# Attention and two mixture-of-experts layers on one core: second-layer products at other places of the second MoE's steps, with the banks swapped from step to step

## The chip, the cores and the metric

One core of a Trainium2 chip. The metric is the device time of the whole program in microseconds (us). The core's engines run beside each other, each through its own list of instructions in order: PE (TensorE, matrix products into the accumulators, PSUM), DVE (VectorE), ACT (ScalarE), POOL (GpSimd) and SP (SyncE, which issues the transfers). They wait for each other at semaphores.

## The reference

```
x = attention(q, k, v)                     # 4 x 576 tokens, 8 heads of 64; to (2304, 512)
p = domain_probs / (domain_probs.sum(-1) + 1e-9)
y = 0
for e in range(4):                         # first MoE: 512 -> 1024 -> 512
    y += p[:, e:e+1] * (relu(x @ w1[e]) @ w2[e])
h = y @ w_in                               # second MoE: 512 -> 2048 -> 512
g = where(h > 0, h, exp(min(h, 0)) - 1)    # ELU
out = g @ w_out
```

All in fp32. The kernel writes each factor as a sum of a high and a low part and forms hi\*hi, hi\*lo and lo\*hi, three matrix products for one.

## The kernel before

Expert 0 runs beside the attention. The rest is a list of 30 *steps*, `STEPS` = (s, b): s counts ten slices of 512 hidden units (s = 0 to 5 the first MoE, 6 to 9 the second; `S_MOE` = 6), b three blocks of 768 tokens. The step with number i = 3s + b forms the *first layer* of its slice and block, and between its products the *second layer* of the step before, i - 1.

**First layer** (`product`, `PRODUCTS`, L1146). A 2 x 2 block product by Strassen's scheme in Winograd's form: seven products, done for two halves of the slice (`fp` 0 and 1), so 14 products a step, numbered 0 to 13 (`idx = 7 * fp + p`), each of six 128x128x384 matmuls. Each half has four PSUM banks A to D. Product 0 goes to C, from which ACT takes a copy `s5` (L1424). Product 1 goes to B, and ACT copies B to A (L1427, "the copy to A" below). Product 2 adds to B, so it must not start before that copy has read B. Then DVE writes D = B + s5 (L1431), product 3 adds to A, product 4 to B, DVE writes C = B + s5 (L1442), product 5 adds to D, product 6 to B. So A, C, D and B end in turn as the four quarters A11, A22, A21, A12 of the hidden layer. The second half's bank D is the bank that the next step's product 1 overwrites. In `fp` 1 the same things happen at products 7 to 13: product 8 is followed by the copy to A, and 9 waits for it.

**ELU** (`elu`, second MoE). For a quarter, ACT does three operations (L1184 to L1186) and, later in the order, `rest()` does two on DVE (L1193, L1194; the second reads the bank). After A21, `rest()` also forms the sums S1, S2, S3 (L1198 to L1200) and after A12 S4 (L1203), which the second layer's seven-product scheme needs. Each result is split in a high part by ACT (L1168) and a low part by POOL (L1169). `run_pend()` is where the DVE part is put in the order: at product 4, 5, 6 and the next half's 0, or earlier, at product 3 or 10, if a second-layer product stands behind that one (`if idx in fill: run_pend()`).

**Second layer.** For s = 7, 8, 9 it has seven *turned products* T0 to T6 (`turned_product`, `TURNED`, L1272), of twelve matmuls each, into two pairs of PSUM banks called X and Y, which they use in turn: T0, T2, T4, T6 go to Y and T1, T3, T5 to X. T0, T1 and T5 start a pair afresh, the others add to what is there. Behind each, DVE adds the pair to the result in SBUF (L1281, "the add"); the next product of the same pair must not start before that add has read it. In the order of DVE the add stands behind what the next first-layer product brings (`flush_adds()`). `PLACES` = (1, 2, 4, 6, 8, 10, 12) says behind which first-layer products T0 to T6 stand. For s = 6 the second layer is eight plain groups (`group`, `GROUP_PLACES`), for s = 5 six chunks (`chunk`).

**Weights.** Some 24 small jobs a step, the *hooks*, prepare the next weights: `MIXED` and `PLAIN` say how many of them have been put into the order by the end of each product (hooks 2 and 3 behind product 1, hooks 10 to 12 behind 6, and so on). For s > 6 `w2_fast` holds the second-layer weights' sums (`w2_sum`, DVE, L807) and splits (`w2_parts`, ACT L798 and POOL L799), and `w1_steps` the first layer's: `hi` on ACT (L757), `lo` and `sums1` on DVE (L768, L773, L774) or POOL, `sums2` on POOL. Steps with b = 0 carry most of `w2_fast` and the second half of `w1_steps`, b = 1 the end of `w2_fast`, b = 2 the first half of `w1_steps` for the next s. The last step has no hooks. The instructions of each engine stand in the order in which this code emits them; nothing moves them later.

Of the kernel before, what the change touches and what calls it, by code (L numbers as in the profile page):

```python
# [21 lines left out]
def tile_attention_moe_moe(  # L22
# [50 lines left out]
    def cut(*sizes):  # L73
# [5 lines left out]
    TB, FS = 384, 4  # L79
    NB = NT // (2 * TB)  # L80
    STEPS = [(s, b) for s in range((NU - 1) * FPU // FS) for b in range(NB)]
    S_MOE = (E - 1) * FPU // FS
# [19 lines left out]


    TURNED = (
        ("A11", "B11", "Y", (0, 0)), ("S1", "T1", "X", (1, 1)), ("S2", "T2", "Y", (0, 1)), ("S4", "B22", "X", (0, 1)),
        ("S3", "T3", "Y", (1, 1)), ("A12", "B21", "X", (0, 0)), ("A22", "T4", "Y", (1, 0)),
    )
    STARTS, ENDS = (0, 1, 5), (3, 4, 5, 6)
    GROUPS = tuple((th, m) for th in (1, 0) for m in range(4))
    GROUP_PLACES = (2, 3, 4, 6, 8, 9, 11, 12)  # L110

    const = ctx.enter_context(tc.tile_pool(name="const", bufs=1))
    big = ctx.enter_context(tc.tile_pool(name="big", bufs=1))
# [624 lines left out]
    def w1_steps(s, p):  # L738

        r, t = [], []  # L740

        def begin():
            r.append(w1r.pop((s, p)).rearrange("p j (d f) -> p j d f", d=KD))
            for _ in range(4):
                t.append(wp.tile([P, 2, KD, P], F32R, tag="w1", name="w1s"))
            if s % 2:
                t[0], t[2] = t[2], t[0]
            hi(0)

# [25 lines left out]

        def sums2():
            f1, f2 = r[0][:, 0], r[0][:, 1]
            nc.gpsimd.tensor_tensor(out=f2[:, 2:], in0=f2[:, 2:], in1=f1[:, :2], op=ALU.subtract)
            nc.gpsimd.tensor_tensor(out=f1[:, 2:], in0=f1[:, 2:], in1=f2[:, 2:], op=ALU.subtract)

        return {
            -5: begin, -4: lambda: lo(0), -2: sums1, -1: lambda: hi(1), 0: lambda: lo(1), 1: sums2,
            5: lambda: hi(2), 6: lambda: lo(2), 8: lambda: hi(3), 9: lambda: lo(3),
        }
# [24 lines left out]
    def w2_fast(i, s, d):  # L809

        for k, fn, op in (
            (8, w2_parts, "B11"), (14, w2_sum, "T1"), (16, w2_parts, "T1"), (18, w2_parts, "B22"), (19, w2_sum, "T3"),
            (21, w2_parts, "B21"), (25, w2_sum, "T2"), (27, w2_parts, "T2"), (30, w2_parts, "T3"), (31, w2_sum, "T4"),
            (34, w2_parts, "T4"),
        ) if s > S_MOE else (
            (8, w2_parts, "B11"), (13, w2_sum, "T1"), (17, w2_parts, "T1"), (18, w2_parts, "B22"), (19, w2_sum, "T3"),
            (21, w2_parts, "B21"), (22, w2_parts, "T3"), (24, w2_sum, "T2"), (26, w2_parts, "T2"), (27, w2_sum, "T4"),
            (30, w2_parts, "T4"),
        ):
            put = lambda k, fn: at2(i, k, fn) if k >= 0 else at(210 + k, fn)  # L820
            put(k - d, lambda fn=fn, op=op: fn(s, op))
# [55 lines left out]
    for i, (s, b) in enumerate(STEPS):  # L877
# [7 lines left out]
        if b == 0:  # L885
# [11 lines left out]
            if s == S_MOE:  # L897
                a1, b1 = (42, 42)
            elif s > S_MOE:
                a1, b1 = (34, 39)  # L900
            if more and not SEVEN[s] and not SEVEN[s + 1]:
                at2(i, a2, lambda s=s: w_load(s + 1, 0, 1))
                at2(i, b2, lambda s=s: w_load(s + 1, 1, 1))
# [353 lines left out]
    def turned_product(i, k, last=False):  # L1257
# [3 lines left out]
            for n in "XY":  # L1261
                sums[n] = bank("o")
        s, b = STEPS[i]
        op, wname, x, (th, mh) = TURNED[k]
        t, y = w2g[s, wname], sums[x][:, :, :TB]
        for m in range(2):
            n = 0
            for fp in range(2):
# [69 lines left out]
    def second_product(i, k):  # L1338
# [60 lines left out]
    pieces = [piece for u, bi, (f,) in pending for piece in second_(u, bi, f)]  # L1399

    for i, (s, b) in enumerate(STEPS):
        fill = {}
        if fast(i - 1):
            one = turned_product if turned(i - 1) else second_product
            fill = {n: (one, i - 1, k) for k, n in enumerate(PLACES)}
        elif turned(i - 1):
            fill = {n: (group, i - 1, *g) for g, n in zip(GROUPS, GROUP_PLACES)}
        elif i > 0:
            fill = {n: (chunk, i - 1, c) for c, n in zip(CHUNKS, (1, 3, 5, 8, 10, 12))}
        hooks = MIXED if fast(i - 1) or turned(i - 1) else PLAIN  # L1410
        if i + 1 == len(STEPS):
            hooks = {}
        for fp in range(2):
            A_, B_, C_, D_ = (A, B, C, D) if fp == 0 else (C, D, A, B)
            banks = {"A": A_, "B": B_, "C": C_, "D": D_}
            f1, f2 = 2 * fp, 2 * fp + 1
            moe = s < S_MOE
            for p in range(len(PRODUCTS)):
                idx = 7 * fp + p
                goal[0] = i * SH + hooks[idx] if idx in hooks else hook2_n[0]  # L1420
# [121 lines left out]
```

## Time and profile before

| | us |
|---|---|
| median of 3 runs | 1254.12 (1252.95 to 1254.65) |
| the profiled execution's own time | 1253.47 |
| its span | 1251.6 |

The profiled execution is one run, and the span is what its trace covers; 1.9 us lie around it. All moments below count from the start of the span. The first layer of the step with s = 6, b = 0 begins at 801.7, the first step that carries turned products (s = 7, b = 1) at 953.4; the last step ends at 1226.1, and behind it stand the last seven turned products alone. A matmul's end is modelled in the trace, so a product's length is best read from start to start.

### The profile page before, as it was taken

The numbers are of one execution on the slowest core, as the hardware profiler recorded it, in microseconds if no ns is written. First come the engines' busy times: TensorE is split into PE (matmuls) and PEld (weight loads), VectorE is DVE, ScalarE is ACT, GpSimd is POOL, SyncE is SP. The second block draws the span as 40 slices with busy tenths as digits, with TensorE's granted clock in tenths as the row PEclk, the third lists the DMA queues.
The fourth block names the chain that finished last, engine by engine and source line by source line (L and its number), as shares of the span: only waits on it lengthen the run. The fifth ranks groups of instructions, "written<-read, shape, count | busy, mean of one in ns | idle before, by whom it ended". The sixth has DMA issues, their size and how long they took to land.

```text
span 1251.6 us, 21084 instructions
## 1 busy us (share of the span) xinstructions
PE 1184.6 (95%) x7516; PEld 1126.3 (90%) x7516; DVE 906.8 (72%) x1516; ACT 676.1 (54%) x1430; POOL 651.1 (52%) x611
## 2 busy tenths in 40 slices
PE   7799999999999999999999999978999988989897
PEld 6788889889999999999999998868999977988897
DVE  6877887565877887877877865655557788787774
ACT  6544543244455554454554534546777656665662
POOL 4522552046476476575584632536247557556652
PEclk9999999999999999999999999989999989999898
DMA  9345557837777767676766679978655554644152
GB/s 268 109 143 171 187 196 245 307 116 258 251 254 253 248 243 261 224 247 241 245 247 244 218 279 325 322 233 262 239 182 193 206 194 168 231 157 173 53 225 89
DMA packets 157400, 272.35 MB, mean 218 GB/s; under 512 B 12784, under 2 KB 83952, under 8 KB 157296
## 3 DMA queue, kind: packets, MB, share of 16 engines
q1 hardware_dynamic: 155568, 267.87, 62.5%
q10 hardware_dynamic: 1728, 3.15, 0.7%
q8 instruction: 59, 0.97, 0.3%
q14 instruction: 45, 0.37, 0.1%
HBM read 224.83 MB, written 46.14 MB: 216 GB/s over the span
## 4 chain that ended last, share of the span: by engine, by line
PE 73%; DVE 12%; ACT 7%; issue 3%; DMA 3%; POOL 2%; SPq 0%; DVEq 0%; ACTq 0%; POOLq 0%
PE o L1361 18%; PE h L1146 13%; PE m L1146 13%; PE o L1272 7%; PE h L1005 7%; PE o L1005 6%; ACT half L1185 1%; DVE gt L1199 1%; DVE accs L1281 1%; DVE extra L1193 1%; PE o L1245 1%; PE o L1247 1%; PE o L1246 1%; DVE half L1200 1%; DVE half L1194 1%
## 5 line engine op out<-in xcount | busy, mean ns | idle before, releaser
L1146 PE MATMUL m<-xh,w1s 128*128 128x384 f32 x840 | 250.0, 341 | 12.1 <-DVE half L1194 7.8
L1146 PE MATMUL h<-xh,w1s 128*128 128x384 f32 x840 | 244.6, 337 | 9.9 <-DVE half L1194 6.2
L1146 PEld LDWEIGHTS m<-xh,w1s 128*128 128x128 f32 x840 | 156.3, 190 | 20.6 <-DVE half L1194 10.6
L1146 PEld LDWEIGHTS h<-xh,w1s 128*128 128x128 f32 x840 | 155.4, 189 | 12.5 <-DVE half L1194 6.5
L1146 PE MATMUL m<-xl,w1s 128*128 128x384 f32 x420 | 141.8, 338 | 0.0
L1146 PE MATMUL h<-xl,w1s 128*128 128x384 f32 x420 | 141.1, 336 | 0.0
L1005 PE MATMUL o<-w2t,hpa 128*128 128x512 f32 x432 | 118.4, 401 | 0.8 <-DVE hpa L1037 0.5
L1005 PE MATMUL h<-xh,w1t 128*128 128x256 f32 (+1 forms) x512 | 112.0, 297 | 0.1
L1005 PEld LDWEIGHTS h<-xh,w1t 128*128 128x128 f32 x512 | 86.1, 192 | 5.2 <-POOL w1t L442 0.3
L1361 PE MATMUL o<-w2g,xh 128*128 128x256 f32 x540 | 90.4, 282 | 0.0
L799 POOL TENSOR_TENSOR w2g<-r,w2g 128x512 fp32r<-128x512 f32 x56 | 75.8, 1362 | 26.1 <-ACT w2g L798 26.1
L1005 PEld LDWEIGHTS o<-w2t,hpa 128*128 128x128 f32 x432 | 75.6, 189 | 14.9 <-DVE hpa L1037 2.4
L1361 PE MATMUL o<-w2g,hpa 128*128 128x256 f32 x540 | 89.0, 282 | 0.0
L1361 PE MATMUL o<-w2g,xl 128*128 128x256 f32 x540 | 87.3, 282 | 0.0
L1383 DVE SCALAR_TENSOR_TENSOR accs<-o,pn,accs 128x256 f32<-128x256 f32 x180 | 75.7, 474 | 14.8 <-PE o L1361 14.2
L1146 PEld LDWEIGHTS m<-xl,w1s 128*128 128x128 f32 x420 | 79.8, 190 | 0.4
L1146 PEld LDWEIGHTS h<-xl,w1s 128*128 128x128 f32 x420 | 79.5, 189 | 0.5
L1361 PEld LDWEIGHTS o<-w2g,xh 128*128 128x128 f32 x540 | 78.0, 190 | 0.1
L1005 PE MATMUL h<-xl,w1t 128*128 128x256 f32 (+1 forms) x256 | 77.3, 302 | 0.0
L1361 PEld LDWEIGHTS o<-w2g,hpa 128*128 128x128 f32 x540 | 76.1, 190 | 0.1
L1361 PEld LDWEIGHTS o<-w2g,xl 128*128 128x128 f32 x540 | 75.6, 190 | 0.2
L1272 PE MATMUL o<-hpa,w2g 128*128 128x384 f32 x216 | 53.5, 366 | 19.9 <-DVE accs L1281 19.9
(301 smaller groups left out, 3033.7 us busy)
## 6 DMA issues: line engine op xcount, KB each, us to landing
xh<-xs SPq DMA_DIRECT2D x210, 384.0 KB, 5.3
xl<-xs SPq DMA_DIRECT2D x210, 384.0 KB, 6.0
r<-in_w_dram SPq DMA_DIRECT2D x56, 256.0 KB, 4.7
xs<-stage SPq DMA_DIRECT2D x43, 256.0 KB, 3.1
xs<-xh SPq DMA_DIRECT2D x21, 384.0 KB, 4.1
xs<-xl SPq DMA_DIRECT2D x21, 384.0 KB, 4.1
r<-scratch SPq DMA_DIRECT2D x24, 256.0 KB, 4.1
x<-in_w_in_dram SPq DMA_DIRECT2D x10, 512.0 KB, 3.8
```

Of the source, the lines that this page charges most:

```text
L799: nc.gpsimd.tensor_tensor(out=t[:, 1], in0=src, in1=t[:, 0].bitcast(F32), op=ALU.subtract)
L1005: nc.tensor.matmul(out, lhsT, rhs, **kw)
L1146: nc.tensor.matmul(dst, t[:, wl, c + dl, :], x[xl_][:, dl, :], start=(n == 0 and p < 2), stop=(n == 5), skip_group_check=True,)
L1185: nc.scalar.activation(out=t, in_=m, func=AF.Tanh, scale=-0.5)
L1193: nc.vector.scalar_tensor_tensor(out=m, in0=m, scalar=1.0, in1=t, op0=ALU.add, op1=ALU.mult)
L1194: nc.vector.scalar_tensor_tensor(out=g, in0=h, scalar=0.0, in1=m, op0=ALU.max, op1=ALU.add)
L1199: tt(out=s2, in0=s1, in1=g11, op=ALU.subtract)
L1200: tt(out=g21, in0=g21, in1=g11, op=ALU.subtract)
L1245: nc.tensor.matmul(o, w[:, 0, :], gh, start=(f == 0), stop=False)
L1272: nc.tensor.matmul(y[:, m], l, r, start=(n == 0 and k in STARTS), stop=(n == 5), skip_group_check=True)
L1361: nc.tensor.matmul(o, l, r, start=(first_write and m == 0 and c != 1), stop=(m == 5), skip_group_check=True)
L1383: nc.vector.scalar_tensor_tensor(out=a, in0=sums[x][:, c * HALF_M : (c + 1) * HALF_M], scalar=pr, in1=a, op0=ALU.mult, op1=ALU.add)
```

## The change

1. The turned products' places become (0, 2, 3, 5, 7, 9, 12). The first MoE keeps `PLACES`.
2. The pair of banks is no longer fixed to a product but goes by `(i + k) % 2`, so that T6 of one step and T0 of the next use different pairs.
3. The groups of s = 6 go to (2, 3, 4, 5, 7, 9, 10, 12), and the chunks in the first step of s = 6 to (0, 2, 5, 7, 9, 12), with a hook table `EARLY` that follows them.
4. For s > 6 some weight jobs move by one hook: the sum T1 from 14 to 13 and its split from 16 to 17, the sum T2 from 25 to 24 and its split from 27 to 28, T4's sum ahead of T3's split, T4's split and the loads one later; in `w1_steps` all `lo` jobs and `sums2` one later.

```
-        ("A11", "B11", "Y", (0, 0)), ("S1", "T1", "X", (1, 1)), ...
+        ("A11", "B11", (0, 0)), ("S1", "T1", (1, 1)), ...
-    GROUP_PLACES = (2, 3, 4, 6, 8, 9, 11, 12)
+    GROUP_PLACES, TURNED_PLACES = (2, 3, 4, 5, 7, 9, 10, 12), (0, 2, 3, 5, 7, 9, 12)
...
+        if s > S_MOE:
+            return {
+                -5: begin, -3: lambda: lo(0), -2: sums1, -1: lambda: hi(1), 1: lambda: lo(1), 2: sums2,
+                5: lambda: hi(2), 7: lambda: lo(2), 8: lambda: hi(3), 10: lambda: lo(3),
+            }
         return {
             -5: begin, -4: lambda: lo(0), -2: sums1, -1: lambda: hi(1), 0: lambda: lo(1), 1: sums2,
             5: lambda: hi(2), 6: lambda: lo(2), 8: lambda: hi(3), 9: lambda: lo(3),
...
-            (8, w2_parts, "B11"), (14, w2_sum, "T1"), (16, w2_parts, "T1"), (18, w2_parts, "B22"), (19, w2_sum, "T3"),
-            (21, w2_parts, "B21"), (25, w2_sum, "T2"), (27, w2_parts, "T2"), (30, w2_parts, "T3"), (31, w2_sum, "T4"),
-            (34, w2_parts, "T4"),
+            (8, w2_parts, "B11"), (13, w2_sum, "T1"), (17, w2_parts, "T1"), (18, w2_parts, "B22"), (19, w2_sum, "T3"),
+            (21, w2_parts, "B21"), (24, w2_sum, "T2"), (28, w2_parts, "T2"), (30, w2_sum, "T4"), (31, w2_parts, "T3"),
+            (35, w2_parts, "T4"),
...
-        op, wname, x, (th, mh) = TURNED[k]
-        t, y = w2g[s, wname], sums[x][:, :, :TB]
+        op, wname, (th, mh) = TURNED[k]
+        t, y = w2g[s, wname], sums["XY"[(i + k) % 2]][:, :, :TB]
...
+    EARLY = {0: 4, 2: 8, 5: 12, 7: 16, 9: 20, 12: 24}
     PLAIN, MIXED = ({1: 4, 3: 8, 5: 12, 8: 16, 10: 20, 12: 24}, {
...
+            one, places = (turned_product, TURNED_PLACES) if turned(i - 1) else (second_product, PLACES)
+            fill = {n: (one, i - 1, k) for k, n in enumerate(places)}
...
-            fill = {n: (chunk, i - 1, c) for c, n in zip(CHUNKS, (1, 3, 5, 8, 10, 12))}
-        hooks = MIXED if fast(i - 1) or turned(i - 1) else PLAIN
+            fill = {n: (chunk, i - 1, c) for c, n in zip(CHUNKS, (1, 3, 5, 8, 10, 12) if moe else (0, 2, 5, 7, 9, 12))}
+        hooks = MIXED if fast(i - 1) or turned(i - 1) else PLAIN if moe else EARLY
```

What this moves, at three places. Lines of the changed kernel lie five lower from the middle on (L1277 is before's L1272, L1151 is L1146, L1286 is L1281, L1436 is L1431, L1447 is L1442, L1198 and L1199 are L1193 and L1194, L812 is L807).

PE, before, at the start of the last step: the end of product 0 (`m_2900`), product 1 (`m_2899`), T0 (`o_10012`, pair Y) and the first matmul of product 2:

```order
L1146 MATMUL m_2900<-xh_90,w1s_11258 128x384
L1146 MATMUL m_2899<-xh_90,w1s_11260 128x384
L1146 MATMUL m_2899<-xl_91,w1s_11260 128x384
L1146 MATMUL m_2899<-xh_90,w1s_11260 128x384 x2
L1146 MATMUL m_2899<-xl_91,w1s_11260 128x384
L1146 MATMUL m_2899<-xh_90,w1s_11260 128x384
L1272 MATMUL o_10012<-hpa_93,w2g_11565 128x384 x3
L1272 MATMUL o_10012<-gx_94,w2g_11565 128x384 x3
L1272 MATMUL o_10012<-hpa_93,w2g_11565 128x384 x3
L1272 MATMUL o_10012<-gx_94,w2g_11565 128x384 x3
L1146 MATMUL m_2899<-xh_90,w1s_11258 128x384
```

The same place now:

```order
L1151 MATMUL m_2900<-xh_90,w1s_11259 128x384
L1277 MATMUL o_9999<-hpa_93,w2g_11566 128x384 x3
L1277 MATMUL o_9999<-gx_94,w2g_11566 128x384 x3
L1277 MATMUL o_9999<-hpa_93,w2g_11566 128x384 x3
L1277 MATMUL o_9999<-gx_94,w2g_11566 128x384 x3
L1151 MATMUL m_2899<-xh_90,w1s_11261 128x384
L1151 MATMUL m_2899<-xl_91,w1s_11261 128x384
L1151 MATMUL m_2899<-xh_90,w1s_11261 128x384 x2
L1151 MATMUL m_2899<-xl_91,w1s_11261 128x384
L1151 MATMUL m_2899<-xh_90,w1s_11261 128x384
L1151 MATMUL m_2899<-xh_90,w1s_11259 128x384
```

T0 has moved ahead of product 1, and products 1 and 2, both in `m_2899`, now follow each other directly.

PE, before, the turned product T6 of the step ahead of that, with the end of product 12 and the start of product 13:

```order
L1146 MATMUL m_2899<-xh_90,w1s_11411 128x384
L1272 MATMUL o_10012<-xh_90,w2g_11910 128x384 x3
L1272 MATMUL o_10012<-hpa_93,w2g_11910 128x384 x3
L1272 MATMUL o_10012<-xh_90,w2g_11910 128x384 x3
L1272 MATMUL o_10012<-hpa_93,w2g_11910 128x384 x3
L1146 MATMUL h_2898<-xh_90,w1s_11409 128x384
```

And now:

```order
L1151 MATMUL m_2899<-xh_90,w1s_11410 128x384
L1277 MATMUL o_10000<-xh_90,w2g_11912 128x384 x3
L1277 MATMUL o_10000<-hpa_93,w2g_11912 128x384 x3
L1277 MATMUL o_10000<-xh_90,w2g_11912 128x384 x3
L1277 MATMUL o_10000<-hpa_93,w2g_11912 128x384 x3
L1151 MATMUL h_2898<-xh_90,w1s_11408 128x384
```

Before, T6 and the next T0 both write `o_10012`; now T6 writes `o_10000` and T0 `o_9999`.

DVE, before, in the first half of the step with s = 9, b = 1 (L1431 belongs to product 2, L1442 to product 4, `gt<-h` and `gt<-m` are the ends of A11 and A22, L807 is the weights' sum T4):

```order
L1431 TENSOR_TENSOR h<-m,extra 128x384
L1281 TENSOR_TENSOR accs<-o,accs 128x768 x2
L1442 TENSOR_TENSOR m<-m,extra 128x384
L1193 SCALAR_TENSOR_TENSOR extra<-extra,half 128x384
L1194 SCALAR_TENSOR_TENSOR gt<-h,extra 128x384
L807 TENSOR_TENSOR r<-r 128x512
L1193 SCALAR_TENSOR_TENSOR half<-half 128x384
L1194 SCALAR_TENSOR_TENSOR gt<-m,half 128x384
L1281 TENSOR_TENSOR accs<-o,accs 128x768
```

The same place now:

```order
L1286 TENSOR_TENSOR accs<-o,accs 128x768
L1436 TENSOR_TENSOR h<-m,extra 128x384
L1198 SCALAR_TENSOR_TENSOR extra<-extra,half 128x384
L1199 SCALAR_TENSOR_TENSOR gt<-h,extra 128x384
L1286 TENSOR_TENSOR accs<-o,accs 128x768
L812 TENSOR_TENSOR r<-r 128x512
L1447 TENSOR_TENSOR m<-m,extra 128x384
L1286 TENSOR_TENSOR accs<-o,accs 128x768
L1198 SCALAR_TENSOR_TENSOR half<-half 128x384
L1199 SCALAR_TENSOR_TENSOR gt<-m,half 128x384
```

A second-layer product stands behind product 3 now and none behind 10. So in the first half A11's DVE part, the add of T1 and here the sum T4 come ahead of C = B + s5 (L1447); in the second half C = B + s5 comes first.

## Rows read from the trace of the kernel before

**Rows 1.** The page: span, and busy time of each engine.

```profile
span 1251.6 us, 21084 instructions
...
PE 1184.6 (95%) x7516; PEld 1126.3 (90%) x7516; DVE 906.8 (72%) x1516; ACT 676.1 (54%) x1430; POOL 651.1 (52%) x611
```

**Rows 2.** Waits of PE, 780 to 1252: waiter, awaited: total us, times, longest.

```profile
PE o L1272 <- DVE accs L1281: 22.1, 10, 3.9
...
PE h L1146 <- ACT m L1427: 3.7, 3, 1.8
```

**Rows 3.** Windows, one a step: length, busy by engine, PE clock, DMA share, GB/s.

```profile
953.42:983.13 29.71, 29.56 (x170) 29.09 (x169) 24.72 (x35) 21.23 (x45) 21.26 (x18) 1.00 0.52 179
...
1015.76:1053.01 37.25, 32.06 (x170) 31.01 (x169) 29.26 (x42) 23.03 (x49) 24.12 (x21) 0.91 0.49 175
1053.01:1089.16 36.15, 31.79 (x169) 31.14 (x169) 26.45 (x38) 22.99 (x49) 22.31 (x19) 0.91 0.46 158
1089.16:1121.79 32.63, 29.99 (x170) 29.02 (x169) 27.12 (x41) 21.40 (x46) 17.39 (x16) 1.00 0.55 196
...
1194.85:1226.06 31.21, 29.67 (x169) 28.87 (x168) 22.26 (x35) 20.11 (x43) 15.83 (x14) 1.00 0.49 189
```

**Rows 4.** Timeline, end of a b = 1 step: start, length, engine, line, idle before.

```profile
1085.20 0.57 DVE L1442 TENSOR_TENSOR h<-h,extra 128x384 f32<-128x384 f32 x1
...
1086.04 2.24 PE L1272 MATMUL o<-xh,w2g 128*128 128x384 f32 x12
...
1093.19 0.48 ACT L1427 ACTIVATE h<-m 128x384 f32<-128x384 f32 x1
...
1093.22 0.81 PE L1272 MATMUL o<-hpa,w2g 128*128 128x384 f32 x3 [1.27 <-DVE accs L1281]
```

**Rows 5.** Timeline, end of a b = 0 step.

```profile
1049.89 0.68 PE L1272 MATMUL o<-gx,w2g 128*128 128x384 f32 x3
...
1055.70 1.62 POOL L799 TENSOR_TENSOR w2g<-r,w2g 128x512 fp32r<-128x512 f32 x1
...
1056.21 1.52 DVE L1199 TENSOR_TENSOR gt<-gt 128x384 f32<-128x384 f32 x1
...
1059.89 0.48 ACT L1427 ACTIVATE h<-m 128x384 f32<-128x384 f32 x1
...
1059.92 1.33 PE L1272 MATMUL o<-hpa,w2g 128*128 128x384 f32 x3 [3.01 <-DVE accs L1281]
```

**Rows 6.** Timeline, step of s = 6: product 2 right behind product 1.

```profile
887.20 0.44 PE L1146 MATMUL m<-xh,w1s 128*128 128x384 f32 x1 [0.96 <-DVE half L1194]
...
888.56 0.47 ACT L1427 ACTIVATE h<-m 128x384 f32<-128x384 f32 x1 [0.47 <-PE m L1146]
...
889.09 0.44 PE L1146 MATMUL m<-xh,w1s 128*128 128x384 f32 x1 [0.56 <-ACT h L1427]
```

**Rows 7.** Groups by line, 963 to 1230: busy, mean ns, idle before.

```profile
L798 ACT ACTIVATE w2g<-r 128x512 fp32r<-128x512 f32 x16 | 9.9, 618 | 2.5 <-DVE r L807 2.5
...
L1281 DVE TENSOR_TENSOR accs<-o,accs 128x768 f32<-128x768 f32 x54 | 51.2, 948 | 4.1 <-PE o L1272 4.1
...
L807 DVE TENSOR_TENSOR r<-r 128x512 f32<-128x512 f32 x9 | 9.6, 1065 | 0.0
...
L1194 DVE SCALAR_TENSOR_TENSOR gt<-m,half 128x384 f32<-128x384 f32 x8 | 4.5, 557 | 0.3
...
L1185 ACT ACTIVATE half<-extra 128x384 f32<-128x384 f32 x32 | 16.8, 526 | 1.0
```

**Rows 8.** Timeline, product 8 of the first step of s = 6.

```profile
828.23 0.69 PE L1146 MATMUL h<-xh,w1s 128*128 128x384 f32 x1 [6.21 <-DVE half L1194]
```

**Rows 9.** Timeline, T0 behind the last step.

```profile
1230.11 1.33 PE L1272 MATMUL o<-hpa,w2g 128*128 128x384 f32 x3 [3.89 <-DVE accs L1281]
```

**Rows 10.** Windows right behind two waits of PE.

```profile
941.85:945.85 4.00, 4.00 (x23) 4.00 (x24) 1.89 (x4) 1.87 (x5) 2.37 (x3) 1.00 0.93 315
1059.90:1064.00 4.10, 4.08 (x13) 4.08 (x14) 2.15 (x4) 1.94 (x5) 3.01 (x3) 0.50 0.01 2
```

More of the change, by code (lines that the diff above doesn't have):

```diff
@@ L104, in tile_attention_moe_moe @@
     TURNED = (
-        ("A11", "B11", "Y", (0, 0)), ("S1", "T1", "X", (1, 1)), ("S2", "T2", "Y", (0, 1)), ("S4", "B22", "X", (0, 1)),
-        ("S3", "T3", "Y", (1, 1)), ("A12", "B21", "X", (0, 0)), ("A22", "T4", "Y", (1, 0)),
+        ("A11", "B11", (0, 0)), ("S1", "T1", (1, 1)), ("S2", "T2", (0, 1)), ("S4", "B22", (0, 1)),
+        ("S3", "T3", (1, 1)), ("A12", "B21", (0, 0)), ("A22", "T4", (1, 0)),
     )
@@ L899, in tile_attention_moe_moe @@
             elif s > S_MOE:
-                a1, b1 = (34, 39)
+                a1, b1 = (35, 40)
             if more and not SEVEN[s] and not SEVEN[s + 1]:
@@ L1401, in tile_attention_moe_moe @@
     for i, (s, b) in enumerate(STEPS):
-        fill = {}
+        moe, fill = s < S_MOE, {}
         if fast(i - 1):
-            one = turned_product if turned(i - 1) else second_product
-            fill = {n: (one, i - 1, k) for k, n in enumerate(PLACES)}
+            one, places = (turned_product, TURNED_PLACES) if turned(i - 1) else (second_product, PLACES)
+            fill = {n: (one, i - 1, k) for k, n in enumerate(places)}
         elif turned(i - 1):
@@ L1416, in tile_attention_moe_moe @@
             f1, f2 = 2 * fp, 2 * fp + 1
-            moe = s < S_MOE
             for p in range(len(PRODUCTS)):
```

## The prediction

> **What bounds the kernel now.** The page first: the span is 1251.6, PE is busy for 95% of it and DVE for 72% [rows 1]. So PE sets the time, and what it waits for comes next. From 780 on the waits of PE name one pair above all: the turned products wait 22.1 in ten cases for the add L1281, up to 3.9 each; products that wait for the copy to A are few (3.7 in three) [rows 2]. The reader should then see where the waits lie, step by step. A turned product takes 2.08 and a first-layer product 1.04 (T6 starts at 1086.04 and the next step at 1089.16, with T6 and product 13 between, so 3.12 for eighteen equal matmuls) [rows 3, 4]. A step of fourteen and seven is 29.12. The eight steps with turned products take 29.71 (the first, b = 1), 32.63 (b = 2), 37.25 (b = 0), 36.15 (b = 1), 32.63, 37 and 36 again (within 0.5), and 31.21 (the last): 272.6 in all, as 953.42 to 1226.06 says, 39.7 above eight times 29.12 [rows 3].
>
> The boundary of two steps shows why. In a light one product 12 ends at 1086.04, where T6 starts. T0 of the next step could start 5.2 later (T6 and three products) and starts at 1093.22, 7.18 later, since the add of T6 stands in DVE's order behind the sums of A21 [rows 4]. Behind a b = 0 step it is 10.03 (1049.89 to 1059.92) [rows 5], and the PE clock is then 0.50, 1.2 GHz, for four us: 12 matmuls take about 4 in place of 2.08 [rows 10]. That is what the 0.91 of these steps is [rows 3].
>
> **The swapped pairs and T0 behind product 0.** T0 now writes the pair that T5 left, whose add is ahead of A21's sums, so T0's wait goes, at eight boundaries, and also product 1's, as T0 stands ahead of it. T1 meets T6's add instead; that add is done about 10.0 after product 12 even in the heavy case [rows 5], and T1 comes behind product 2, later than that (below). What is late next is product 2: it must not start before the copy to A, and now nothing stands between product 1 and it. ACT is in order, and the copy starts 7.15 after product 12's end in the light case (1093.19) and 10.00 in the heavy one (1059.89), 0.48 long [rows 4, 5]. The new order brings PE to the end of product 1 after T6, 13, 0, T0, 1: 7.28. Light: the copy follows product 1 at once. What that costs stands in a step of s = 6, where the two already are neighbours: from product 1's start at 887.20 to product 2's at 889.09, 1.89 in place of 1.04 [rows 6], 0.85. Heavy: product 2 starts at about 10.55, 3.27 late. I take 0.85 four times and 3.3 four times; the lower bound for the heavy ones is 0.85, if ACT is on time there.
>
> **Products 8 and 9.** The same neighbours stand in the second half, and there the copy is behind a longer chain. From L1442 to the next copy to A it is 7.99 in the light case (1085.20 to 1093.19) [rows 4]: ELU of three quarters and the splits, one after the other on ACT. With the start of L1442 0.2 behind product 4 and 0.54 for the copy and PE's start, product 9 can begin 8.73 after product 4's end. Between them PE now has products 5, 6, 7, 8, T3, T4: 8.32. L1442 is later too: at product 3 A11's DVE part and T1's add now come ahead of it. After product 3 ACT needs 0.2 + three times 0.53, DVE two times 0.6 and 0.95 [rows 7]: 3.95, against 3.12 for T2 and product 4, with 0.2 again: about 0.7 to 0.9 late. So product 9 waits 1.3 in a light half. Each split or `hi` that the hooks put on ACT there adds its 0.62 [rows 7]: two in b = 0 and in b = 1; in b = 2 two of the first layer's, one half as wide, taken as 1.0. In b = 1 the sum T4 also stands ahead of L1442, one L807, 1.07 [rows 7]. So 1.3 (last), 2.3 (b = 2), 2.55 (b = 0), 3.55 (b = 1). Bounds: 0.85 each, as in rows 6, and another 1 where a T2 or T3 split, now nearer to its use, is late.
>
> One row bears on b = 0: L1199, A21's sum, takes 1.52 where POOL's L799 runs from 1055.70 on [rows 5]. The like DVE operations take 0.56 [rows 7]. A split that starts before the sums holds them up; the last `lo` now stands behind A21's splits in the first half of b = 0 and behind A21's in b = 2, so I count no hold-up there, while B21's split stays where it was. The Trainium skill, SBUF — State Buffer, section "Who interferes with whom", says it as a rule: a VectorE instruction with two SBUF inputs and a GpSimd instruction that reads SBUF exclude each other, and whichever starts first holds the port for its whole length. By that rule the 1.52 here is no accident, and the trace agrees; were the `lo` still first in b = 0, the sum below would be about 1.9 higher (0.96 for each of two steps).
>
> **Sum for the eight steps.** 29.12 + first wait + second wait: first step 29.12 + 0.85 + 3.55 = 33.5; b = 2: 29.12 + 0.85 + 2.3 = 32.3, twice; b = 0: 29.12 + 3.3 + 2.55 = 35.0, twice; b = 1: 29.12 + 3.3 + 3.55 = 36.0, twice; last 31.3. Together 271.4, against 272.6: -1.2. The waits are moved more than removed.
>
> **The clock.** Before, four boundaries were followed by four us at 0.50; behind the wait of 1.8 at 941.85 the clock stayed at 1.00 [rows 2, 10]. The slow T0s came after 3.0 and a shorter wait of product 1 just ahead [rows 10]. The new single wait of 3.3 lies between. A fall costs half of 4.1, 2.05. None is 0, all four heavy ones 8.2; the sum above holds none. I add 3.0, less than half, since 3.3 is the upper end of that wait.
>
> The Trainium skill, TensorE: Matmul & The Clock Gate, Part 1, says that idleness closes the gate and sustained work opens it. By that rule a wait in one piece is worse than the same wait in two. The trace has only the two-piece case at this place, and the page would make it nearer to 8 than to 3: the sum would be 5 higher.
>
> **The tail.** Behind the last step T0 waits 3.89 and starts slow (1.33 for three matmuls) [rows 9]. Now T0 can run in that gap, and T1 takes its place at the add of T6: 2.08 less, and 2 more if the clock stays. I take -3.5, between -2.1 and -4.5.
>
> **The chunk step and the groups.** In the first step of s = 6 product 8 waits 6.21 for the end of A21 [rows 8]. Now a chunk of twelve 128x512 matmuls stands ahead of it, 2.8 (twelve matmuls a third longer than a turned product's), which fills a part. DVE's work there, which sets the 6.21, is the same list, and waits for its own transfers. Against it stand two new neighbour pairs, 0.85 each, and for it product 1, no longer first behind the last reader of its bank. I take -2.5, from -6 to +2. The groups get one new pair (8, 9) in each of three steps, 0.85, of which one waited already: +1.7, and -1.0 for the `lo` behind the sums: +0.7.
>
> **Sum.** -1.2 + 3.0 - 3.5 - 2.5 + 0.7 = -3.5. The profiled execution took 1253.47, which is 0.65 under the median of the runs and inside their range. 1253.5 - 3.5 = 1250.0.
>
> **Rivals.** (1) ACT is on time and both waits are 0.85 everywhere, because sums now stand four hooks ahead of the splits that ACT would have stood still for (2.5 at L798 [rows 7]). For it: ACT is busy only some 23 of 36 us in these steps [rows 3]. Against: it is a chain, not a load. The heavy first waits alone are 4 x 2.45 = 9.8, and no clock falls (3.0): 1237. In the extreme, all waits 0.85: 8 x 30.8 = 246.6, 1253.5 - 26 - 5.3 = 1222. Chance 0.22. (2) The other side: the clock falls behind every wait of some 3 us. Place: products 2 and 9; price 2.05 each, at four heavy boundaries and in three b = 1 steps, 14.4 in place of 3.0: 1261.4. It decides from the point where a single wait passes about 3. For it: [rows 10]. Against: 1.8 did nothing, and the b = 1 waits may be nearer 2.5. Chance 0.22. (3) The trade is even: the copy waits take what T0's waits gave, the tail and the chunk are worth 2: 1253.5, which reads as if the change did nothing. Should T1 really meet T6's add, it ends here too. Chance 0.2. The forecast has 0.36, with a range of its own of 1246 to 1253.
>
> **Chances and range.** About 0.2%, 2.5 us, is what can be told from no change: under 1251.6 is faster, over 1256.6 slower. The forecast gives 0.27 faster and 0.09 the same; (1) 0.22 faster; (2) 0.22 slower; (3) 0.01 faster, 0.16 the same, 0.03 slower. Faster 0.50, same 0.25, slower 0.25. The range runs from the start of (1), 1238, to the half of (2), 1259.
>
> **What would show it.** No wait of T0 for L1281 inside the steps, and at the tail the wait at T1. Waits of products 2 and 9 for L1427 in all eight steps, the largest at b = 1. L1199 near 0.56 in the first half of b = 0. Steps of 35, 36 and 32.3. In the tail the last product less than 21 after 1226. It is wrong if the copy waits stay under 1 (rival 1), if 0.50 stands behind them (rival 2), or if T1, T2 or T4 waits for L1281 or for L799.

## The result and the profile after

The changed kernel takes 1266.86 us (median of four runs, 1265.34 to 1267.46). The ratio to the kernel before is 1.0101, with a 95% interval of 1.0083 to 1.0118: it is slower by 1%. The prediction said 1250.0 and a range of 1238 to 1259. It was wrong in sign and in range.

The page of the changed kernel, span and busy time, to be read against [rows 1]:

```profile
span 1263.6 us, 21088 instructions
...
PE 1194.2 (95%) x7516; PEld 1133.2 (90%) x7516; DVE 895.4 (71%) x1516; ACT 676.7 (54%) x1430; POOL 651.0 (52%) x611
```

PE executes the same 7516 matmuls, but is busy for 9.6 longer (1184.6 to 1194.2), while the span grew by 12.0. So four fifths of the loss is no idle time at all: the same number of matmuls takes longer. Only 2.4 is added waiting.

The waits of PE from 780 on (waiter, awaited: total, times, longest), against [rows 2]:

```profile
PE m L1151 <- ACT h L1432: 17.5, 11, 4.5
PE h L1151 <- ACT m L1432: 13.6, 12, 1.8
PE o L1277 <- DVE accs L1286: 5.2, 4, 1.8
PE m L1151 <- DVE half L1199: 5.1, 3, 2.3
PE h L1151 <- DVE m L1436: 3.7, 2, 1.9
...
PE o L1277 <- POOL w2g L804: 1.9, 3, 0.7
```

The 22.1 for the add have become 5.2. In their place products 2 and 9 wait for the copy to A (L1432 now), 31.1 together, of which 7.9 lie in the steps of s = 6. Two names are new: the DVE write D = B + s5 (L1436) and a weight split on POOL (L804). The end of an ELU quarter (L1199) was waited for before as well, as L1194, 6.2 at product 8 [rows 8] and otherwise this:

```profile
PE m L1146 <- DVE half L1194: 7.8, 9, 1.4
```

Now its cases are fewer, and the longest is 2.3.

One window a step, from the first step with turned products (b = 1, 2, 0, 1) and the last one (columns as in [rows 3]):

```profile
958.70:992.88 34.18, 30.37 (x169) 28.98 (x169) 24.44 (x37) 22.42 (x48) 21.39 (x19) 1.00 0.52 199
992.88:1028.35 35.47, 31.59 (x170) 30.63 (x169) 26.94 (x43) 23.00 (x49) 17.84 (x17) 0.95 0.59 202
1028.35:1064.23 35.88, 31.57 (x169) 30.55 (x169) 26.34 (x39) 21.48 (x47) 23.03 (x20) 0.95 0.36 114
1064.23:1102.07 37.84, 32.55 (x170) 31.59 (x169) 25.66 (x39) 22.94 (x48) 22.71 (x20) 0.91 0.52 194
1211.27:1242.19 30.92, 29.72 (x170) 29.08 (x169) 21.18 (x35) 20.09 (x43) 15.87 (x14) 1.00 0.42 163
```

Of the next three the lengths are 35.50, 35.84 and 37.86, so each kind repeats. Shorter are b = 0 (37.25 to 35.88) and the last step by 0.3; b = 2 grew by 2.8, b = 1 by 1.7, the very first step by 4.5. All eight in one window, first of the kernel before, then of the changed one:

```profile
953.42:1226.06 272.64, 246.53 (x1345) 239.92 (x1344) 212.66 (x308) 176.21 (x369) 164.77 (x142) 0.96 0.48 170
```

```profile
958.70:1242.19 283.49, 251.56 (x1346) 243.69 (x1345) 203.51 (x310) 177.34 (x372) 164.47 (x143) 0.95 0.47 168
```

The difference of the first two numbers is PE's idle time: 26.1 before, 31.9 after. The eight steps lost 10.9: 5.8 in waits and 5.0 in slower matmuls. The four steps ahead of them (called the steps of s = 6 here: the three of s = 6 and s = 7, b = 0) lost 5.3 (150.7 to 155.9), and the tail gained 4.1 (25.5 to 21.4). The s = 6 steps in one window, before and after:

```profile
802.75:953.42 150.67, 134.63 (x729) 127.59 (x729) 83.74 (x132) 97.60 (x208) 73.92 (x77) 0.97 0.72 242
```

```profile
802.77:958.70 155.93, 139.80 (x729) 131.76 (x729) 81.97 (x130) 97.34 (x205) 73.73 (x76) 0.93 0.68 226
```

There the idle time is the same, 16.0 and 16.1. The whole loss is in PE's busy time (134.6 to 139.8), at a lower granted clock.

Three places show the new waits. First the start of a b = 1 step, where product 2 waits for the copy, and the first matmuls of T1 behind it:

```profile
1071.19 0.48 ACT L1432 ACTIVATE h<-m 128x384 f32<-128x384 f32 x1
...
1071.72 0.69 PE L1151 MATMUL m<-xh,w1s 128*128 128x384 f32 x1 [3.16 <-ACT h L1432]
...
1073.81 1.16 PE L1277 MATMUL o<-hpa,w2g 128*128 128x384 f32 x3
```

Three matmuls took 1.16 where the same three take 0.68 at full speed [rows 5]: the granted clock behind this wait is 0.50, 1.2 GHz. Second, product 11 in a b = 2 step:

```profile
1019.79 1.13 DVE L768 TENSOR_TENSOR w1s<-r,w1s 128x256 fp32r<-128x256 f32 x1
...
1020.85 0.55 DVE L1436 TENSOR_TENSOR m<-h,extra 128x384 f32<-128x384 f32 x1
...
1021.45 0.44 PE L1151 MATMUL h<-xh,w1s 128*128 128x384 f32 x1 [1.86 <-DVE m L1436]
```

The instruction right ahead of L1436 on DVE is a `lo` job of the first-layer weights (L768), which the change put one hook later. Third, product 1 in a step with groups, and the DVE operation that it waits for:

```profile
887.44 0.56 DVE L1199 SCALAR_TENSOR_TENSOR half<-m,extra 128x384 f32<-128x384 f32 x1
...
888.05 0.44 PE L1151 MATMUL m<-xh,w1s 128*128 128x384 f32 x1 [2.26 <-DVE half L1199]
```

The bank of product 1 is the one from which A21's ELU reads; before, the same wait was 0.96 [rows 6].

### The profile page after: what moved, and what is told of

The parts are those of the page before. It is cut to its first block, busy times and chain, and to the rows that moved or that the text cites. A ratio compares the mean times of both kernels' runs of the same rounds, so it can differ in the third digit from the quotient of the medians.

```text
span 1263.6 us, 21088 instructions
## 1 busy us (share of the span) xinstructions
PE 1194.2 (95%) x7516; PEld 1133.2 (90%) x7516; DVE 895.4 (71%) x1516; ACT 676.7 (54%) x1430; POOL 651.0 (52%) x611
## 4 chain that ended last, share of the span: by engine, by line
PE 70%; DVE 10%; ACT 9%; issue 4%; POOL 3%; DMA 3%; SPq 1%; DVEq 0%; ACTq 0%; POOLq 0%
PE o L1366 18%; PE m L1151 14%; PE h L1151 13%; PE h L1010 6%; PE o L1010 6%; PE o L1277 4%; ACT half L1190 2%; DVE extra L1198 1%; PE o L1251 1%; PE o L1250 1%; PE o L1252 1%; ACT extra L1191 1%; DVE half L1199 1%; ACT extra L1189 1%; DVE gt L1204 1%
## 5 line engine op out<-in xcount | busy, mean ns | idle before, releaser
L1151 PE MATMUL m<-xh,w1s 128*128 128x384 f32 x840 | 254.8, 346 | 24.3 <-ACT h L1432 17.5
L1151 PE MATMUL h<-xh,w1s 128*128 128x384 f32 x840 | 247.9, 339 | 17.9 <-ACT m L1432 13.6
L1151 PEld LDWEIGHTS m<-xh,w1s 128*128 128x128 f32 x840 | 158.7, 193 | 33.2 <-ACT h L1432 21.0
L1151 PEld LDWEIGHTS h<-xh,w1s 128*128 128x128 f32 x840 | 155.8, 189 | 23.8 <-ACT m L1432 17.8
L1151 PE MATMUL m<-xl,w1s 128*128 128x384 f32 x420 | 143.9, 343 | 0.0
L1151 PE MATMUL h<-xl,w1s 128*128 128x384 f32 x420 | 141.4, 337 | 0.0
L804 POOL TENSOR_TENSOR w2g<-r,w2g 128x512 fp32r<-128x512 f32 x56 | 76.9, 1382 | 19.4 <-ACT w2g L803 19.3
L1198 DVE SCALAR_TENSOR_TENSOR extra<-extra,half 128x384 f32<-128x384 f32 x48 | 28.2, 588 | 76.0 <-ACT extra L1191 75.6
L1151 PEld LDWEIGHTS m<-xl,w1s 128*128 128x128 f32 x420 | 81.1, 193 | 0.5
L1151 PEld LDWEIGHTS h<-xl,w1s 128*128 128x128 f32 x420 | 79.5, 189 | 0.4
```

The costliest lines, as they stand in the source:

```text
L804: nc.gpsimd.tensor_tensor(out=t[:, 1], in0=src, in1=t[:, 0].bitcast(F32), op=ALU.subtract)
L1151: nc.tensor.matmul(dst, t[:, wl, c + dl, :], x[xl_][:, dl, :], start=(n == 0 and p < 2), stop=(n == 5), skip_group_check=True,)
L1198: nc.vector.scalar_tensor_tensor(out=m, in0=m, scalar=1.0, in1=t, op0=ALU.add, op1=ALU.mult)
```

## The experiments

All were timed against runs of the kernel before on the same chip; those runs' medians are 1254.2 to 1255.3, so a difference of 1 or 2 between two experiments says little. Lengths of steps and windows come from each kernel's own trace.

**1. The swapped pairs alone**, on the kernel before, with its places, groups and weight jobs:

```
-        t, y = w2g[s, wname], sums[x][:, :, :TB]
+        t, y = w2g[s, wname], sums["XY"[(i + k) % 2]][:, :, :TB]
```

> The kernel before with one edit: the pair of banks goes by (i + k) % 2; places, groups, chunks and hooks as before. Theory 1 (the swap is good by itself, the loss is in the places): T0's waits for the add go, and product 2, which T0 still covers, starts where the copy to A ends: 1.7 us earlier in the light boundaries, 3.4 in the four heavy ones, no slow clock behind them, about 3 less in the tail: 1232 to 1238. Rival (the copy to A is as late as the add was, so the swap is worth nothing wherever T0 stands): 1248 to 1254.

Measured: 1232.92, ratio 0.9825 (0.98 to 0.9851). The theory held; the rival fell. This one line gives the fastest of all the versions here (experiment 12, which contains it, is not told apart from it). The page, the waits from 952 on, and the eight steps in one window:

```profile
PE 1174.4 (95%) x7516; PEld 1117.5 (91%) x7516; DVE 906.8 (74%) x1516; ACT 676.4 (55%) x1430; POOL 653.4 (53%) x611
```

```profile
PE m L1146 <- ACT h L1427: 6.5, 4, 1.8
PE m L1146 <- DVE half L1194: 5.8, 7, 1.3
PE o L1272 <- DVE accs L1281: 4.4, 4, 1.8
PE h L1146 <- ACT m L1427: 1.9, 2, 0.9
...
```

```profile
953.77:1208.33 254.56, 237.99 (x1345) 232.43 (x1345) 213.51 (x308) 176.26 (x369) 165.10 (x142) 1.00 0.52 181
```

18.1 less than before in the eight steps: 9.5 of it idle time (26.1 to 16.6), 8.5 slow matmuls (246.5 to 238.0). The granted clock is 1.00 throughout, and yet PE is busy for 5.0 more than eight times 29.12 (233.0): that much is no clock but the slow start of a product behind each of 16 waits, about 0.3 a wait (in [rows 6] it is 1.89 against 1.04 with a wait of 0.56, so 0.29). So what followed had to be lost by the rest of the change: 34 us.

**2. The changed kernel with the old places of the turned products:**

```
-    GROUP_PLACES, TURNED_PLACES = (2, 3, 4, 5, 7, 9, 10, 12), (0, 2, 3, 5, 7, 9, 12)
+    GROUP_PLACES, TURNED_PLACES = (2, 3, 4, 5, 7, 9, 10, 12), (1, 2, 4, 6, 8, 10, 12)
```

> The changed kernel with the turned products back at (1, 2, 4, 6, 8, 10, 12); swapped banks, new groups, chunks and hooks kept. Theory 1 (places): products 2 and 9 no longer stand bare behind the copy, so the 10.9 us that the eight steps had gained go, and what the swap gives shows: 1236 to 1246. Rival (the moved hooks make DVE and ACT late): stays above 1255, and product 11 still waits for L1436 in steps of b = 2.

Measured: 1240.84, 0.9881 (0.9855 to 0.9907), 26.0 less than the changed kernel. The eight steps are 258.1. The places are the main loss, and with the old ones product 11 does not wait for L1436, although the `lo` stands where the change put it: it takes both.

**3. The changed kernel with the old groups, chunks and `PLAIN`:**

```
-    GROUP_PLACES, TURNED_PLACES = (2, 3, 4, 5, 7, 9, 10, 12), ...
+    GROUP_PLACES, TURNED_PLACES = (2, 3, 4, 6, 8, 9, 11, 12), ...
-            ... zip(CHUNKS, (1, 3, 5, 8, 10, 12) if moe else (0, 2, 5, 7, 9, 12))}
-        hooks = MIXED if fast(i - 1) or turned(i - 1) else PLAIN if moe else EARLY
+            ... zip(CHUNKS, (1, 3, 5, 8, 10, 12))}
+        hooks = MIXED if fast(i - 1) or turned(i - 1) else PLAIN
```

> The changed kernel with the groups of s = 6 and the chunks of its first step where they were, and no EARLY table. If the 5.3 us that the four steps of s = 6 have gained come from these places alone: 1260 to 1263, product 1 of the second and third group step waits about 1 us again instead of 2.3, product 8 of the first step waits about 6 again. If they come from the hooks (which fall in these steps too): 1266 to 1268.

Measured: 1259.11, 1.0039 (1.0025 to 1.0052), a little under what was expected. The steps of s = 6 take 150.05 in place of 155.93: all of their loss is back. Product 1 waits under 1.0 again, and product 8 has its 6.2 again.

**4. The changed kernel with all weight jobs of before** (`w2_fast`, `w1_steps`, `a1, b1`):

```
-        if s > S_MOE:
+        if False:
...
-            (8, w2_parts, "B11"), (13, w2_sum, "T1"), (17, w2_parts, "T1"), ...
+            (8, w2_parts, "B11"), (14, w2_sum, "T1"), (16, w2_parts, "T1"), ...
```

> The changed kernel with w2_fast, w1_steps and the loads at their hooks of before; places and banks as changed. Theory 1 (places): 1264 to 1269, the waits for the copy stay. Rival (hooks): product 11's wait for L1436 in b = 2 goes, steps of b = 1 lose their extra, 1256 to 1260.

Measured: 1259.51, 1.0035 (1.0018 to 1.0051). The theory that the jobs are worth nothing fell, and the rival was right: beside the new places the moved jobs cost 7.4. b = 2 falls from 35.5 to 32.6 and b = 1 from 37.8 to 33.6, but b = 0 rises from 35.9 to 39.5.

**5. The swapped pairs and all seven new places**, groups and jobs of before:

```
-            fill = {n: (one, i - 1, k) for k, n in enumerate(PLACES)}
+            fill = {n: (one, i - 1, k) for k, n in enumerate((0, 2, 3, 5, 7, 9, 12) if turned(i - 1) else PLACES)}
```

> The kernel before with the swapped banks and the turned products at (0, 2, 3, 5, 7, 9, 12); groups, chunks and hooks of before. Theory (the places alone cost, by leaving products 2 and 9 bare behind the copy to A, product 9 behind a chain that starts late): 20 to 24 over the kernel with the swap alone (1232.9), so 1253 to 1257, with the steps of b = 0 at 39 to 40 as in the changed kernel with the old hooks. Rival (the places hurt only together with the moved hooks or the groups): under 1242.

Measured: 1251.54, 0.9979 (0.9963 to 0.9995). The theory was 1.5 too high, the rival fell. The trace is of the slowest of its ten runs (1256.58), so its parts are larger than those of a median run. Its eight steps, and its waits from 952 on:

```profile
955.22:1232.98 277.76, 249.91 (x1345) 242.55 (x1345) 203.66 (x308) 176.76 (x369) 163.33 (x142) 0.96 0.49 167
```

```profile
PE h L1146 <- ACT m L1427: 13.8, 8, 3.6
PE m L1146 <- ACT h L1427: 11.8, 8, 2.4
...
```

Against experiment 1 the places alone add 23.2 to the eight steps of this run, 11.3 idle and 11.9 slow matmuls; between the medians they add 18.6.

**6, 7 and 8. Parts of the places**, on the kernel of experiment 1. Each is the edit of 5 with other numbers:

```
6: (0, 2, 4, 6, 8, 10, 12)      # T0 moved alone
7: (1, 2, 4, 6, 7, 9, 12)       # T4 and T5 moved
8: (1, 2, 3, 5, 8, 10, 12)      # T2 and T3 moved
```

> The kernel before with the swapped banks and only T0 moved, to behind product 0. Copy theory: product 2 starts where the copy to A ends, with T0 ahead of product 1 or behind it; product 1's wait for A21's end (some 6 us in all) goes, and product 2's bare wait of 0.85 comes in the light boundaries: 1231 to 1236, next to the swap alone. Rival (a bare product 2 is dear in itself): 1240 or more.

> The kernel before with the swapped banks and only the second half's T4 and T5 moved, to behind products 7 and 9. Copy theory: product 9 is bare, but the chain on ACT starts early, so 0.85 a step and some more where hooks are on ACT: 1239 to 1245. Rival (all the cost is product 9's bareness): 1250 or more.

> The kernel before with the swapped banks and only the first half's T2 and T3 moved, to behind products 3 and 5. Copy theory: C = B + s5 comes later in DVE's order and 2 us nearer to product 5, so the ACT chain starts late and ends 1.2 to 3.5 behind product 8 and T4: 1246 to 1254, the dearest of the three moves. Rival (only bare neighbours cost, and T4 still covers 8 and 9): 1232 to 1236.

Measured: 1241.05 (0.9894, 0.9878 to 0.9911), 1242.33 (0.9904, 0.9884 to 0.9923) and 1249.13 (0.9958, 0.9943 to 0.9973). All three lose against 1232.92: 8.1, 9.4 and 16.2. They don't add up: together they lose 18.6. 6 missed its theory, and the time is the rival's (1240 or more): the waits of products 1 and 2 became one wait of product 2 of 3.1 to 3.2, and the clock fell behind three of its four cases (0.68, 0.57 and 0.64). The third and the fourth, and the four us behind each:

```profile
1124.33 0.69 PE L1146 MATMUL m<-xh,w1s 128*128 128x384 f32 x1 [3.20 <-ACT h L1427]
...
1159.46 0.44 PE L1146 MATMUL m<-xh,w1s 128*128 128x384 f32 x1 [3.08 <-ACT h L1427]
```

```profile
1124.33:1128.33 4.00, 4.00 (x15) 4.00 (x16) 2.60 (x5) 1.57 (x3) 3.09 (x5) 0.64 0.51 180
...
1159.46:1163.46 4.00, 4.00 (x23) 4.00 (x24) 3.61 (x6) 1.46 (x3) 2.91 (x4) 1.00 0.02 6
```

7 came as expected (product 9 waits in all eight steps, 5.3 in all). 8 came in time, but not where it was placed: product 8 waits for the end of A21's ELU. T2 stands ahead of product 4 there, in place of behind it. C = B + s5 starts behind product 4, and the ELU of A22 and A21 behind C, so PE has one turned product less (2.08) to do between it and product 8. In a b = 0 step C also starts later, 1.25 behind the end of product 4 (1034.53 against 1033.28) where it is 0.20 in experiment 1 (1027.64 against 1027.44), since a turned product behind product 3 puts A11's DVE part ahead of it. Why product 1 waits longer as well is not shown. Its waits from 952 on (the m rows are product 1's, which were 5.8 in experiment 1):

```profile
PE h L1146 <- DVE half L1194: 8.4, 8, 2.3
PE m L1146 <- DVE half L1194: 8.1, 7, 2.5
...
```

**9 and 10. Half of the weight jobs each**, on the changed kernel: 9 has the first-layer jobs of before (`if False:` in `w1_steps`), 10 the second-layer jobs and loads.

> The changed kernel with the first-layer weight jobs (w1_steps) of before, and the second-layer weight jobs as changed. Theory: of the moved jobs it is the second lo, one hook later, that stands ahead of D = B + s5 (L1436) in the second half of a b = 2 step. Product 11's wait of 1.86 goes, both b = 2 steps fall from 35.5 to 32.6 (-5.8), b = 1 stays near 37.8, and a b = 0 step gains or loses what the last lo does ahead of A21's sums (L1203 up to 1.5 in place of 0.56, up to +3.6 each): 1261 to 1268 against 1266.9. Rival, that the second-layer jobs make the whole difference: no step changes by more than 0.5, 1266 to 1268, and product 11 still waits.

> The changed kernel with the second-layer weight jobs (w2_fast, and the loads) of before, and the first-layer jobs as changed. Theory: T4's sum (L812) no longer stands ahead of C = B + s5 (L1447) in a b = 1 step, and T3's split comes one hook earlier: the b = 1 steps fall from 37.8 to 33.6 (-8.4), T4 no longer waits for L804, b = 2 stays at 35.5 with product 11's wait: 1257 to 1260. Rival, that all of the hooks' 7.4 came from the first-layer jobs: 1264 to 1268.

Measured: 1263.98 (1.0093, 1.0066 to 1.0119) and 1260.57 (1.0059, 1.0037 to 1.0082). The theory of 9 holds in time; that of 10 (1257 to 1260) was missed by 0.6, and its rival is farther off. In 9 product 11's wait falls from 1.86 to at most 0.6 and the b = 2 steps to 32.6, while b = 0 rises to 40.4 and 37.9: the later `lo` jobs harm b = 2 and help b = 0. Its b = 1 steps fall too, to about 36.8 and 35.4, where the theory had them stay. In 10 no turned product waits for L804 any more, and product 11 waits as in the changed kernel. Its b = 1 steps fell less than thought (34.7 and 36.4, not 33.6); its trace is of the slowest of its four runs (1265.18, the others 1259.9 to 1261.2).

**11. A11's DVE part behind C = B + s5**, on the kernel of experiment 5:

```
-                        if idx in fill:
+                        if idx in fill and not fast(i - 1):
                             run_pend()
```

> The kernel before with swapped pairs and all seven turned products at the new places, and A11's two DVE operations put into the order at products 4 and 11, behind C = B + s5 (L1442), in the steps that carry turned products. Theory: product 9's wait of up to 3.6 is a chain that begins with C; with two operations (0.6 each) less ahead of it the chain ends 1 to 1.3 earlier in each half, eight steps become about 1.2 shorter, and where a wait falls under 2 the clock stays up: 1236 to 1245 against 1251.5, b = 0 steps 39.6 to about 37. Rival, that ACT's own chain or the order of A11's splits holds the copy: 1249 to 1253, since A11's split now stands later on ACT ahead of the same copy.

Measured: 1256.97, 1.0016 (0.9999 to 1.0034). Theory refuted, and its rival (1249 to 1253) was missed too. From C to the copy in the same b = 0 step, in 5 and then in 11:

```profile
1036.84 0.56 DVE L1442 TENSOR_TENSOR m<-m,extra 128x384 f32<-128x384 f32 x1
...
1043.96 1.52 DVE L1199 TENSOR_TENSOR gt<-gt 128x384 f32<-128x384 f32 x1
...
1047.58 0.48 ACT L1427 ACTIVATE m<-h 128x384 f32<-128x384 f32 x1
```

```profile
1032.59 0.57 DVE L1442 TENSOR_TENSOR m<-m,extra 128x384 f32<-128x384 f32 x1 [2.34 <-PE m L1146]
...
1039.71 1.53 DVE L1199 TENSOR_TENSOR gt<-gt 128x384 f32<-128x384 f32 x1
...
1043.34 0.48 ACT L1427 ACTIVATE m<-h 128x384 f32<-128x384 f32 x1
```

In 11 C starts as soon as PE lets it, but from there to the copy it is 10.75 in both (1036.84 to 1047.58, 1032.59 to 1043.34). The chain behind C sets the copy, with L1199 at 1.5 in both where the like operations take 0.56. Product 9 still waits 3.0 for it, 0.56 less than in 5; in the b = 2 steps it waits 0.47 less (1.48 to 1.01), but in b = 1 0.58 more (1.18 to 1.76), so that its eight waits are 13.8 in 5 and 13.9 in 11. Why the median of 11 is 5.4 above that of 5 no trace shows: the one of 11 is of nearly its fastest run, the one of 5 of its slowest.

**12. Swapped pairs and the changed chunks** in the first step of s = 6:

```
-            ... zip(CHUNKS, (1, 3, 5, 8, 10, 12))}
+            ... zip(CHUNKS, (1, 3, 5, 8, 10, 12) if s < S_MOE else (0, 2, 5, 7, 9, 12))}
-        hooks = MIXED if fast(i - 1) or turned(i - 1) else PLAIN
+        hooks = MIXED if ... else PLAIN if s < S_MOE else {0: 4, 2: 8, 5: 12, 7: 16, 9: 20, 12: 24}
```

> The kernel before with swapped pairs, and the chunks of the first step of s = 6 at (0, 2, 5, 7, 9, 12) with the hook table of the changed kernel; the groups, turned products and weight jobs are those of before. Theory: that step becomes 1.2 to 2.2 shorter as it did in the changed kernels (43.8 to 41.6 - 42.6), the rest stays: 1230.5 to 1232. Rival, that the next step gives it back (39.2 in place of 38.2 in the changed kernel): 1232.5 to 1233.5.

Measured: 1234.94 (0.9844, 0.9825 to 0.9863; runs from 1231.8 to 1236.3), not told apart from experiment 1 (1231.95 to 1235.34). The first step of s = 6 is 1.6 shorter (42.2 against 43.8), as the theory had it, and the next one 0.5 longer (38.7 against 38.2), half of what the rival had. But three later steps, the last of the s = 6 steps and both b = 0 steps with turned products, are 1.5 to 1.6 longer each, with the same instructions in the same order (the edit moves nothing behind the first step of s = 6). In the first of them product 8 waits 1.86 for the copy and the clock behind it is 0.57; in experiment 1 it waits 1.85 and the clock is 1.00. The trace of 12 is of the slowest of its four runs, that of 1 of the fastest, so this is also how two runs of one kernel can differ. For the first b = 0 step with turned products, the waits at products 1 and 2, and the four us behind them, in 1 and then in 12:

```profile
1016.97 0.45 PE L1146 MATMUL m<-xh,w1s 128*128 128x384 f32 x1 [1.20 <-DVE half L1194]
...
1022.13 0.45 PE L1146 MATMUL m<-xh,w1s 128*128 128x384 f32 x1 [1.74 <-ACT h L1427]
```

```profile
1022.13:1026.13 4.00, 4.00 (x23) 4.00 (x24) 3.16 (x6) 1.57 (x3) 3.09 (x5) 1.00 0.57 186
```

```profile
1018.24 0.44 PE L1146 MATMUL m<-xh,w1s 128*128 128x384 f32 x1 [1.18 <-DVE half L1194]
...
1023.40 0.44 PE L1146 MATMUL m<-xh,w1s 128*128 128x384 f32 x1 [1.76 <-ACT h L1427]
```

```profile
1023.40:1027.40 4.00, 4.00 (x14) 4.00 (x15) 2.59 (x5) 1.57 (x3) 3.09 (x5) 0.59 0.48 183
```

The same two waits within 0.02, and once the clock stays at 1.00, once it falls to 0.59. So a fall is not given by the length of the waits alone.

## Why the prediction was wrong

**The waits of T0: right.** No T0 waits for the add inside the steps, and in the tail T1 does (1.82).

**The copy waits: right in place, too large in sum.** Products 2 and 9 wait in all eight steps. The heavy first wait behind b = 0 was priced at 3.3 and is 3.16. The one behind b = 2 was given the same price without a row of its own and is 1.0. The one of the first step was priced at 0.85 and is 1.89. The second waits are 1.4 to 1.8 and 0.6 in the last step, where 1.3 to 3.55 were set. All sixteen together are 23.2, by estimate 28.0 with 0.3 for each slow start (experiment 1); the sum had 38.4 for them, starts included.

**What the sum did not have: 8.7 of waits at other places.** Product 11 for L1436 (1.86, twice), T3 for the add (1.54, twice), T4 in two b = 1 steps for L804 (0.70 each) and T2 in the first step (0.51). A wait of T2 or T4 for the split was one of the prediction's own signs of being wrong. With the 23.2 that makes the 31.9 idle of the window. With seven starts of 0.3 these places come to 10.8, and the copy waits were 10.4 too high: that the waits come out nearly right in sum is luck. The first is a step that was stated wrongly: the moved `lo` jobs were counted as a gain only (A21's sums at 0.56 in the first half of b = 0, which came true). What the later `lo` now stands ahead of in b = 2 was not asked. Experiments 4 and 9 show that price, 2.9 a step.

**The clock: the step that failed.** The 39.7 above full speed before was 26.1 of idle time and 13.6 of slow matmuls (246.5 against eight times 29.12). The sum replaced all of it by waits and put 3.0 for the clock on top, because four boundaries behind T0's wait were to be freed of it. After, the slow part is 18.6 (251.6 against 233.0). Part of either is slow starts at 0.3 each: 18 waits before, 5.4, and 23 after, 6.9. So by this estimate the clock cost 8.2 before, which is what the prediction read for its four falls, and 11.7 after. The rows of the steps bear it out: a granted clock of 0.95 in four steps of 35.5 to 35.9 and of 0.91 in two of 37.8 is a loss of about 14, with PE's idle time under the lower clock in it. In the eight steps the error is 10.9 + 1.2 - 3.0 = 9.1: waits with their starts 0.4 too low (38.8 against 38.4), clock 8.7 too low (11.7 against 3.0).

The case nearest to what came is rival 2, which took the loss from the clock, priced it at 14.4 and said 1261.4; but it set the fall at single waits of about 3, and of its seven places only the starts of two b = 1 steps had one. The other four falls stand behind product 11 in b = 2 and product 9 in b = 0, so its price is partly luck. These windows of four us stand behind waits of 1.89, 1.86 (the second within 7 us), 1.77 and 3.16:

```profile
965.09:969.09 4.00, 4.00 (x23) 4.00 (x24) 3.06 (x5) 1.46 (x3) 2.90 (x4) 1.00 0.02 4
1021.45:1025.45 4.00, 4.00 (x16) 4.00 (x17) 2.79 (x5) 2.62 (x7) 1.76 (x3) 0.67 0.82 273
1053.17:1057.17 4.00, 4.00 (x14) 4.00 (x15) 3.90 (x5) 0.94 (x2) 4.00 (x4) 0.57 0.00 0
1071.72:1075.72 4.00, 4.00 (x12) 4.00 (x13) 3.06 (x5) 1.46 (x3) 2.90 (x4) 0.50 0.02 6
```

Waits of 1.8 are followed by a fall as well as by none. The prediction had read [rows 10] as "1.8 did nothing" from one case. From the Trainium skill, TensorE: Matmul & The Clock Gate, Part 1, it had drawn that one wait in one piece is worse than the same wait in two. Experiment 6, with one piece, is 8.1 slower than 1, of which 3.1 is longer busy time in the eight steps; but one of its four waits of 3.1 to 3.2 has no fall behind it, and experiment 12 has falls behind two pieces, so the runs don't settle it.

**The trade itself.** The prediction took swap and places as one: T0's waits go, the copy's come. Experiments 1 and 5 part them. The swap alone removes T0's waits and leaves the turned products between products 1 and 2 and between 8 and 9, where they cover the copy; it gains 21. The new places take that cover away and lose 18.6 of it; in the changed kernel, beside the moved jobs and groups, they cost 26.0 (experiment 2). That the swap could be worth so much alone was never priced, since both parts were costed as one row of sums.

**Groups and chunks: wrong.** Set at +0.7 and -2.5, measured +6.5 and -1.2. The group that stood behind product 11 now stands behind 10. C starts behind 11 and A21's ELU follows it, so PE has one group less to do in between, and A11's DVE part now stands ahead of C; product 1 of the next step waits 2.3. That these two make the wait is argued from the order, no run parts them. The sum counted one new pair (8, 9) and no effect across the step's end, and it had no clock term for these steps: of the 6.5, 1.5 is idle time and 5.0 is slower matmuls, at a granted clock of 0.91 to 0.95 where it was 0.96 to 1.00. Experiment 3 gives 5.9 back. Of the chunk, the 6.2 at product 8 did go, and 4.5 came back at product 2 for the copy.

**The tail: right.** -4.1 for -3.5. The profiled execution of the changed kernel (1265.34) is 1.5 under its median.

Open: what decides between 1.00 and a fall behind equal waits. Experiments 1 and 12 show only that it isn't the order of instructions within the step.

## What to carry to other kernels

When a change frees one wait and moves work, cost the two apart: here one line that swaps the banks was worth 21 us, and moving the products gave it away, because they had covered the next wait in the chain. Split the time above full speed into idle and slow matmuls (window length less PE busy, PE busy less matmuls at full clock, with the starts behind waits taken off) before any of it is called a wait; a gap that is only moved can still cost its slow matmuls again. Here 10.2 of the 12.0 are longer busy time, 5.0 in the eight steps and 5.2 in those of s = 6. For every job put later in an in-order queue, name the instruction that it now stands ahead of, in each kind of step, across the step's end too.

## What was not expected of the hardware

The same instructions with waits of 1.20 and 1.74, and of 1.18 and 1.76, were followed by a granted clock of 1.00 in one kernel and 0.59 in another, at the first b = 0 step with turned products of each, and so it goes at the second (1.00 and 0.57). Within one kernel, experiment 6, single waits of 3.20 and 3.08 were followed by 0.64 and 1.00. A fall is about 1.5 a step, and the three that part 12 from 1 have the size of the spread between runs: 1231.8 to 1236.3 of experiment 12, 1248.7 to 1256.6 of experiment 5, 1251.1 to 1259.5 of experiment 11. A comparison of two kernels that differ by 3 us here is partly one of where the clock happened to fall.
